# Attention and mixer in one kernel: lead-in reordered, half sums folded in 14 pairs, drains in a row of GpSimd additions

## The chip, the cores and the metric

The kernel runs on one core of a Trainium2 chip. The metric is the device time of one execution in microseconds (us); lower is better. The engines are called as the profile calls them: PE (TensorE), DVE (VectorE), ACT (ScalarE), POOL (GpSimd) and SP (SyncE, which here only issues DMAs).

## The reference

Two blocks follow each other. q, k, v and the centroids are float32.

- Routing attention: 4 batches, 8 heads, 768 tokens, head dimension 64. Each q and each k is assigned to the one of 16 centroids with the greatest cosine; a query sees only the keys of its own cluster.
- An MLP mixer on the heads put side by side (4 x 768 x 512): one product over tokens (768 to 256 and back), then one over channels (512 to 1536 and back), both with a ReLU and a residual.

```python
mask = q_assign[:, :, :, None] == k_assign[:, :, None, :]
scores = np.where(mask, scale * np.matmul(q, k.transpose(0, 1, 3, 2)), -1e9)
attn = softmax(scores)
x = np.matmul(attn, v)                     # (B,H,S,D), then to (B,S,H*D)
h = np.maximum(x.transpose(0, 2, 1) @ w_tok1, 0.0) @ w_tok2
u = x + h.transpose(0, 2, 1)
out = u + np.maximum(u @ w_ch1, 0.0) @ w_ch2
```

`softmax` stands for the reference's exponential of scores less their greatest, divided by its sum. The weights come as 64-bit floats, which the kernel rounds to 32 bits itself.

## The kernel before, in words

**Order of work.** The kernel adds every operation to a `Program` (L77) with the engines that may do it, a cost for each, and the keys it reads and writes. PE's operations stay in the order in which they are added. For the others a planner (L151) goes forward in planned time and gives each engine, out of what is ready, the operation that is due first; `after` is the planned time before which an operation isn't ready. Due times come from PE's own times going back (L138). So the planned times set only the order of each engine's queue; on the chip each queue runs in its order, with semaphores.

**Lead-in.** `begin` (L944) loads the centroids and the q and k of pairs 0 and 1 and two v, makes an identity matrix on POOL, sets constants, and has PE multiply the identity by itself (`keep_busy`, L1024: 11 times here, each two instructions). The centroids are normalised on DVE and ACT (a square root, and behind it an Exp on one column, L984, which makes ACT load its table for Exp), turned by one PE product, and copied to `cbd`; between the turn and the copies stand 5 more dummy products. `turn_qk` (L1029) turns a pair's q and k by 12 PE products with the identity, in three batches of four, each copied from PSUM to SBUF by ACT (L863) or DVE (L865). `route` (L1071) multiplies the turned q and k with the centroids (four products), then DVE transposes (L1088), takes the maximum (L1089), compares, and transposes back (L1093). For pair 0 the result is placed by eight small instructions (L1114, L1118, L1120, L1125) in a mask operand in SBUF; for the others it goes through ACT (L1097, which also adds up the hits) and three DMAs.

**Attention** goes over 16 pairs of heads. `pair` (L1305) does for each: `scores` (L1150), 12 chunks of two products and two mask products in bfloat16, each chunk then taken by ACT's exponential (L1193) out of one of three sets of two PSUM banks; `values` (L1237), six rounds of 16 products; and the softmax's denominators. For these `add_up` (L1201) adds the exponentials of three key blocks to `es[0]` and of the other three to `es[1]`, four DVE additions of 1536 columns. `sums` (L1251) multiplies them by a matrix of ones in the next pair's values, behind the first round: one set of four products for each of `es[0]` and `es[1]`, or one set in all if the two halves were added first. `FOLD` (L52) has a letter for each pair: `-` is two sets, `V` adds the halves on DVE, `T` adds them by a DMA that POOL issues and that adds to its target (no pair has a `T` before). The q and k of pair 3 and later are turned by DMA transposes, not by PE. In pair 0 PE computes three score chunks ahead, then turns pair 1 and routes it, and only then comes to the mask products; pair 2 is turned and routed after the values of pair 0.

Beside attention, DVE rounds the weights piece by piece (`weight_round`, L1336) and forms sums of blocks of them, which go to DRAM. The loads are planned from `START` = 14 us on, `STEP` = 10 us apart.

**Mixer.** Token and channel products are done by a scheme of seven block products instead of eight. The sums of blocks that it needs are formed on DVE and, in the first channel product, on POOL: a long row of additions of 384 columns (`tt`, L881, with `("POOL",)`).

Of the kernel before, what the change touches and what calls it, by code (L numbers as in the profile page):

```python
# [48 lines left out]
SUM_LO, SUM_HI = 1e-15, 1e15  # L49
GRAIN = 32  # L50
CHECK_AT = 532.0
FOLD = "-VVVVVVVVVV-----"  # L52

# [15 lines left out]
SELF = 0.13  # L69
START, STEP = 14, 10  # L70

# [651 lines left out]
def kernel(  # L723
# [43 lines left out]
    def buf(kb, shape, dt=F32):  # L767
        return Buf(arena, int(kb * 256), shape, dt)
# [31 lines left out]
    qkt = [buf(111 + 3 * i, [NQK, P], U16) for i in range(2)]  # L800
    rb = buf(117, [HS], BF16)
    nsq = buf(118, [P])
    mxs = buf(118.5, [32])
# [65 lines left out]
    def halves(dst, src, n, rd, wr, engines=("ACT",), kind="ACT16"):  # L869
# [9 lines left out]
        )  # L879

    def tt(dst, a, b, op, n, rd, wr, engines=("DVE",)):  # L881
        def fn(e):
            (nc.vector if e == "DVE" else nc.gpsimd).tensor_tensor(out=dst, in0=a, in1=b, op=op)  # L883

        return g.add({e: cost(e, n) for e in engines}, fn, rd, wr)

# [57 lines left out]
    def begin():  # L944
# [3 lines left out]
        load_qk(1, 1.0)  # L948
        load_v(0, 12.0)
        load_v(1, 32.0)  # L950
        g.add({"POOL": 1.0}, lambda e: make_identity(nc, ident.ap), [], ident.k())
# [17 lines left out]
        vec(lambda: nc.vector.memset(M0.ap, 0.0), 0.5, [], M0.k())  # L969
        keep_busy(11)  # L970

# [3 lines left out]
        def norm(e):  # L975
# [7 lines left out]

            nc.scalar.activation(out=col(5), in_=lo, func=ACT.Exp, scale=0.0)  # L984
            for it in range(2):
# [13 lines left out]

        g.add({"DVE": 4.0}, norm, cen.k(), sq.k() + nsq.k())  # L1000
        turn(ps[:, 7, 0:P], sq.ap[:, 0:P], sq.k(), bank(7))
        keep_busy(5)
        for i in range(2):
# [24 lines left out]

    def turn_qk(m, banks):  # L1029
        src, T = qks[m % 2], Ts[m % 3]  # L1030
        for n, bk in enumerate(banks):
            for i in range(4):
                a, j = divmod(4 * n + i, NJ)
                a = 1 - a
                turn(
                    ps[:, bk, i * P : (i + 1) * P],
                    src.ap[:, a, j].rearrange("p h d -> p (h d)"),
                    [("qk", m % 2, a, 0), ("qk", m % 2, a, 1)] + src.rows(a, a + 1), bank(bk),
                )

            copy(
                T.ap[:, 4 * n : 4 * n + 4].rearrange("p a t -> p (a t)"), ps[:, bk], 512,
                bank(bk), T.rows(4 * n, 4 * n + 4),
            )
# [26 lines left out]
    def route(m, bk):  # L1071
# [4 lines left out]
        for gr in range(4):  # L1076
# [5 lines left out]
            )  # L1082
        a, e, o = rt[0:3]

        def blocks(t):
# [7 lines left out]
        vec(lambda: nc.vector.transpose(out=o.ap, in_=e.ap), 0.56, e.k(), o.k())  # L1093

        g.add(
            {"ACT": 0.6},
            lambda e: nc.scalar.activation(  # L1097
                out=rb.ap, in_=o.ap, func=ACT.Identity, scale=msc.ap[:, 0:1],
                bias=msc.ap[:, 1:2], accum_out=hits.ap[:, m : m + 1],
            ),  # L1100
            o.k() + msc.k(), rb.k() + [("hits", m)],
        )
# [47 lines left out]
    def scores(m):  # L1150
# [22 lines left out]
        if m == 0:  # L1173
            turn_qk(1, (7, 6, 7))
            load_qkr(3, 26.0)
            route(1, 6)
        for n in range(2 * NJ):
# [4 lines left out]
            for h in range(2):  # L1182
# [5 lines left out]
                    bank(2 * s + h), pos=(64 * h, 0),  # L1188
                )
            ex = st[i]  # L1190
            g.add(
# [113 lines left out]
    def pair(m):  # L1305
# [3 lines left out]
        if m:  # L1309
            next_qk(m)  # L1310
        for i in range(NJ):
            if i == 4 and 1 <= m < NP - 2:
                route(m + 2, 0)
# [11 lines left out]
        if m == 0:  # L1325
            load_v(2)
            turn_qk(2, (1, 2, 3))
            route(2, 0)
            next_qk(m)
# [614 lines left out]


    begin()
    turn_qk(0, (0, 1, 2))
    load_qk(2, 20.0)
    route(0, 3)
# [83 lines left out]
```

## Time and profile before

| | |
|---|---|
| median of 3 runs | 794.08 us (793.72 to 794.26) |
| profiled execution | 794.77 us, span 793.0 us, granted PE clock 0.999 |
| ACT, busy | 461.2 us (58%) |
| weight loads (PEld), busy | 465.4 us (59%) |
| DMA queue of SP | 141.83 MB, 71.4% of 16 engines' span |
| DMA queue of ACT | 0.79 MB |

The span is the time from the first to the last instruction of the profiled execution. A group of the profile names line, engine, operation, what is written and read, the shapes and the count; then come the busy time, the mean duration of one in ns, and the engine's idle time just before the group with what ended it. A row of the chain of waits or of the timeline starts with the start and the length in us. A row of PE's waits gives the time waited in all, how often, and the longest. Almost every buffer is part of one tile, `arena`, in SBUF, and `ps` is PSUM, so groups are told apart by line and shape. Lines such as L844, L883, L863 or L903 are those of helpers (a product, an addition, a copy, a DMA).

### The profile page before, as it was taken

What the parts mean: (1) busy time and instruction counts of PE and PEld (TensorE: products, weight loads), DVE (VectorE), ACT (ScalarE), POOL (GpSimd) and SP (SyncE); (2) the same over time, 40 slices, a digit from 0 to 9 for tenths busy, and PEclk for the clock granted to TensorE, in tenths of its full rate; (3) what the DMA queues carried; (4) which work ended last, traced back from release to release, by engine and by line L of the source; (5) the groups of instructions that cost most, each with busy time, mean ns of one, the idle gap of its engine ahead of it and who ended that gap; (6) DMA issues with size and microseconds to landing.
All of it is one profiled execution on the core that took longest, in us unless ns stands there. A gap on an engine that the chain in (4) does not pass through costs nothing.

```text
span 793.0 us, 15364 instructions
## 1 busy us (share of the span) xinstructions
PE 780.1 (98%) x5983; PEld 465.4 (59%) x5983; DVE 677.5 (85%) x876; ACT 461.2 (58%) x612; POOL 190.2 (24%) x185
## 2 busy tenths in 40 slices
PE   7999999999999999999999999999999999999997
PEld 6666666666666666544555555555555555555554
DVE  6869999999999999999999967899953567799964
ACT  4688898888898875599714367642245204400422
POOL 0000000000000000001264599700186379830000
PEclk9999999999999999999999999999999999999999
DMA  9576769777678953659858999975788844444767
GB/s 214 154 174 164 183 151 232 205 219 203 162 207 183 273 180 113 182 110 224 184 139 246 312 290 258 270 191 123 167 188 179 170 106 102 100 101 106 162 144 178
DMA packets 326576, 143.68 MB, mean 181 GB/s; under 512 B 260192, under 2 KB 322400, under 8 KB 326496
## 3 DMA queue, kind: packets, MB, share of 16 engines
q1 hardware_dynamic: 324128, 141.83, 71.4%
q8 instruction: 49, 0.80, 0.4%
q10 hardware_dynamic: 2368, 0.79, 0.4%
q14 instruction: 31, 0.25, 0.1%
HBM read 91.95 MB, written 28.61 MB: 152 GB/s over the span
## 4 chain that ended last, share of the span: by engine, by line
PE 88%; DVE 5%; ACT 3%; issue 2%; DMA 1%; SPq 0%; POOL 0%; DVEq 0%; POOLq 0%; ACTq 0%
PE ps L844 72%; PE ps L1226 16%; DVE arena L883 4%; ACT arena L873 2%; DMA wd<-arena 1%; ACT arena L1193 1%; DVE arena L865 0%; DVE arena L1360 0%; SPq L903 0%; DVE arena L1363 0%; ACT arena L863 0%; DVE arena L1366 0%; DVE arena L1356 0%; DVE arena L1280 0%; DVE arena L1273 0%
## 5 line engine op out<-in xcount | busy, mean ns | idle before, releaser
L844 PE MATMUL ps<-arena 128*128 128x384 f32 (+5 forms) x2735 | 642.4, 463 | 7.3 <-DVE arena L865 2.7
L844 PEld LDWEIGHTS ps<-arena 128*128 128x128 f32 (+1 forms) x2351 | 342.3, 185 | 252.8 <-issue 59.5
L883 DVE TENSOR_TENSOR arena<-arena 128x1536 f32<-128x1536 f32 (+6 forms) x350 | 370.2, 1079 | 10.5 <-PE ps L1226 2.3
L883 POOL TENSOR_TENSOR arena<-arena 128x384 f32<-128x384 f32 x179 | 189.5, 1094 | 510.8 <-DVE arena L883 379.4
L883 DVE TENSOR_TENSOR arena<-ps,arena 128x384 f32<-128x384 f32 (+3 forms) x227 | 189.6, 845 | 79.4 <-PE ps L844 75.4
L873 ACT COPY arena<-arena 128x768 uint16<-128x768 uint16 x221 | 189.4, 953 | 61.4 <-DMA arena<-arena 31.9
L1193 ACT ACTIVATE arena<-ps 128x768 f32<-128x768 f32 x192 | 150.6, 811 | 31.6 <-PE ps L844 29.9
L1226 PE MATMUL ps<-arena 128*32 128x192 f32 (+1 forms) x3248 | 144.7, 335 | 0.0
L1226 PEld LDWEIGHTS ps<-arena 128*32 128x32 f32 x3248 | 103.8, 110 | 44.0 <-issue 13.9
L863 ACT COPY arena<-ps 128x384 f32<-128x384 f32 (+2 forms) x41 | 29.5, 728 | 120.6 <-PE ps L844 120.4
L890 ACT ACTIVATE arena<-arena 128x1152 f32<-128x1152 f32 (+1 forms) x38 | 39.9, 1075 | 54.9 <-DVE arena L883 54.5
L1888 ACT ACTIVATE arena<-arena 128x768 f32<-128x768 f32 x40 | 38.7, 970 | 32.7 <-DMA arena<-in_moe_w_ch_dram 24.7
L844 PEld LDWEIGHTS <-arena 64*128 64x128 bf16 x384 | 19.3, 94 | 25.0 <-issue 0.6
L1360 DVE SCALAR_TENSOR_TENSOR arena<-arena 128x512 uint32<-128x512 uint32 (+1 forms) x31 | 20.6, 681 | 0.3
L1097 ACT ACTIVATE arena<-arena 128x384 bf16<-128x384 f32 x16 | 11.2, 703 | 16.1 <-issue 16.1
L1366 DVE SCALAR_TENSOR_TENSOR arena<-arena 128x512 f32<-128x512 uint32 (+1 forms) x31 | 20.2, 671 | 0.4
L1356 DVE TENSOR_SCALAR arena<-arena 128x512 uint32<-128x512 uint32 (+1 forms) x31 | 13.2, 435 | 5.8 <-DMA arena<-in_moe_w_tok_dram 5.8
L1273 DVE STREAM_TRANSPOSE arena<-ps 128x768 f32<-128x768 f32 x16 | 15.3, 955 | 0.0
L1363 DVE TENSOR_SCALAR arena<-arena 128x512 uint32<-128x512 uint32 (+1 forms) x31 | 14.4, 483 | 0.3
L865 DVE COPY arena<-ps 128x384 f32<-128x384 f32 (+3 forms) x12 | 8.0, 666 | 4.7 <-PE ps L844 4.6
L1088 DVE STREAM_TRANSPOSE arena<-ps 128x384 f32<-128x384 f32 x16 | 9.2, 575 | 3.1 <-PE ps L844 3.0
L1280 DVE STREAM_TRANSPOSE arena<-ps 128x384 f32<-128x384 f32 x16 | 9.3, 579 | 1.5 <-PE ps L1226 1.2
(58 smaller groups left out, 53.1 us busy)
## 6 DMA issues: line engine op xcount, KB each, us to landing
arena<-wd SPq DMA_DIRECT2D x196, 192.0 KB, 3.0
wd<-arena SPq DMA_DIRECT2D x84, 224.0 KB, 3.2
arena<-in_moe_w_ch_dram SPq DMA_DIRECT2D x96, 128.0 KB, 3.0
arena<-in_moe_w_ch_dram SPq DMA_DIRECT2D x16, 768.0 KB, 6.0
arena<-in_v_dram SPq DMA_DIRECT2D x16, 384.0 KB, 4.7
out_dram<-arena SPq DMA_DIRECT2D x14, 384.0 KB, 3.6
arena<-in_k_dram SPq DMA_DIRECT2D x13, 384.0 KB, 4.0
arena<-in_q_dram SPq DMA_DIRECT2D x13, 384.0 KB, 4.2
```

The costliest lines, as they stand in the source:

```text
L844: nc.tensor.matmul(dst, lhsT=lhsT, rhs=rhs, start=start, stop=stop, tile_position=pos, is_transpose=tr, skip_group_check=True,)
L863: nc.scalar.copy(out=dst, in_=src)
L873: nc.scalar.copy(out=dst, in_=src)
L883: (nc.vector if e == "DVE" else nc.gpsimd).tensor_tensor(out=dst, in0=a, in1=b, op=op)
L890: nc.scalar.activation(out=dst, in_=src, func=ACT.Relu)
L1193: lambda e, ex=ex, s=s, u=u: nc.scalar.activation(out=ex.ap[:, :, u * HS : (u + 1) * HS], in_=ps[:, 2 * s : 2 * s + 2, 0:HS], func=ACT.Exp ...
L1226: nc.tensor.matmul(dst, lhsT=lhsT, rhs=rhs, start=start, stop=stop, tile_position=pos, skip_group_check=True,)
L1273: lambda: nc.vector.transpose(out=x.ap[:, :, cols].rearrange("p j (c d) -> p c j d", d=32), in_=ps[:, 6:8, 0:HS],),
L1360: vec(lambda: nc.vector.scalar_tensor_tensor(out=TT, in0=hi, scalar=0xC0000000, in1=hh, op0=ALU.bitwise_and, op1=ALU.bitwise_or), 0.14 + 0 ...
L1363: vec(lambda: nc.vector.tensor_scalar(out=hh, in0=TT, scalar1=0xFF800000, scalar2=None, op0=ALU.bitwise_and), f, T.k(), h.k())
L1366: vec(lambda: nc.vector.scalar_tensor_tensor(out=ll, in0=lo, scalar=float(2.0**-52), in1=hh.bitcast(F32), op0=ALU.mult, op1=ALU.mult,), 0. ...
L1888: lambda e, i=i, func=func, bias=bias, n=n, hi=hi: nc.scalar.activation(out=hi, in_=hi, func=func, bias=bias, accum_out=wsum.ap[:, i, n : ...
```

## The change

- The lead-in: 12 dummy products instead of 11, and the 5 further ones are gone; the first two batches of pair 0's turns come before the centroid's turn, the third behind it. The Exp that loads the table comes after the copies of these turns. The routing of pair 1 comes behind the third mask product instead of ahead of the first. Pair 0's row of hits has buffers of its own (`o0`, `rb0`) and is planned at 18 us at the earliest. Pair 2 is turned among the values of pair 0, ahead of the fourth round. The loads of pair 2's q and k, of two v, of pair 3's q and k and of the weights are planned earlier.
- `FOLD`: seven pairs (1, 3, ..., 13) have their halves added by DVE and seven (2, 4, ..., 14) by a DMA; pairs 0 and 15 stay as they are.
- POOL: every second addition whose planned end lies between 435 and 475 us is followed by a drain.

```diff
+BUSY, HITS_AT = 12, 18.0
+LULL = (435.0, 475.0)
-FOLD = "-VVVVVVVVVV-----"
+FOLD = "-VTVTVTVTVTVTVT-"
-START, STEP = 14, 10
+START, STEP = 9, 9
...
+    o0, rb0 = buf(194, [HS]), buf(196, [HS], BF16)
...
+    row = 0
     def tt(dst, a, b, op, n, rd, wr, engines=("DVE",)):
         def fn(e):
+            nonlocal row
             (nc.vector if e == "DVE" else nc.gpsimd).tensor_tensor(out=dst, in0=a, in1=b, op=op)
+            if e == "POOL" and LULL[0] <= o.end < LULL[1]:
+                row += 1
+                if row % 2 == 0:
+                    nc.gpsimd.drain()
...
-        load_v(0, 12.0)
-        load_v(1, 32.0)
+        load_v(0, 9.0)
+        load_v(1, 26.0)
...
-        keep_busy(11)
+        keep_busy(BUSY)
...
-            nc.scalar.activation(out=col(5), in_=lo, func=ACT.Exp, scale=0.0)
...
         g.add({"DVE": 4.0}, norm, cen.k(), sq.k() + nsq.k())
+        turn_qk(0, (0, 1, 2), (0, 1))
         turn(ps[:, 7, 0:P], sq.ap[:, 0:P], sq.k(), bank(7))
-        keep_busy(5)
+        turn_qk(0, (0, 1, 2), (2,))
+        g.add(
+            {"ACT": 1.5},
+            lambda e: nc.scalar.activation(out=col(5), in_=col(1), func=ACT.Exp, scale=0.0),
+            nsq.k() + Ts[0].k(), [("table",)],
+        )
...
+        if m == 0:
+            o = o0
...
+        r = rb if m else rb0
         g.add(
-            {"ACT": 0.6},
+            {"ACT": 0.75},
...
-            o.k() + msc.k(), rb.k() + [("hits", m)],
+            o.k() + msc.k(), r.k() + [("hits", m)], after=0.0 if m else HITS_AT,
...
             turn_qk(1, (7, 6, 7))
-            load_qkr(3, 26.0)
-            route(1, 6)
+            load_qkr(3, 18.0)
...
+            if m == 0 and n == ahead - 1:
+                route(1, 6)
...
         for i in range(NJ):
+            if i == 3 and m == 0:
+                turn_qk(2, (1, 2, 3))
...
             load_v(2)
-            turn_qk(2, (1, 2, 3))
             route(2, 0)
...
     begin()
-    turn_qk(0, (0, 1, 2))
-    load_qk(2, 20.0)
+    load_qk(2, 9.0)
     route(0, 3)
```

More of the change, by code (lines that the diff above doesn't have):

```diff
@@ L879, in halves @@
         )
+    row = 0
     def tt(dst, a, b, op, n, rd, wr, engines=("DVE",)):
         def fn(e):
+            nonlocal row
             (nc.vector if e == "DVE" else nc.gpsimd).tensor_tensor(out=dst, in0=a, in1=b, op=op)
-        return g.add({e: cost(e, n) for e in engines}, fn, rd, wr)
+            if e == "POOL" and LULL[0] <= o.end < LULL[1]:
+                row += 1
+                if row % 2 == 0:
+                    nc.gpsimd.drain()
+        o = g.add({e: cost(e, n) for e in engines}, fn, rd, wr)
+        return o
     def relu(dst, src, n, rd, wr, engines=("ACT", "DVE")):
@@ L1027, in keep_busy, with turn_qk @@
             mm(ps[:, 5, 0:P], ident.ap, ident.ap, True, True, 0.22, ident.k(), bank(5))
-    def turn_qk(m, banks):
+    def turn_qk(m, banks, parts=range(3)):
         src, T = qks[m % 2], Ts[m % 3]
-        for n, bk in enumerate(banks):
+        for n in parts:
+            bk = banks[n]
             for i in range(4):
@@ L1093, in route @@
         vec(lambda: nc.vector.transpose(out=o.ap, in_=e.ap), 0.56, e.k(), o.k())
+        r = rb if m else rb0
         g.add(
-            {"ACT": 0.6},
+            {"ACT": 0.75},
             lambda e: nc.scalar.activation(
-                out=rb.ap, in_=o.ap, func=ACT.Identity, scale=msc.ap[:, 0:1],
+                out=r.ap, in_=o.ap, func=ACT.Identity, scale=msc.ap[:, 0:1],
                 bias=msc.ap[:, 1:2], accum_out=hits.ap[:, m : m + 1],
             ),
-            o.k() + msc.k(), rb.k() + [("hits", m)],
+            o.k() + msc.k(), r.k() + [("hits", m)], after=0.0 if m else HITS_AT,
         )
```

## The prediction

> **What bounds the kernel now.** I read the page first, then PE's list of waits, then three stretches, then the chain of waits in the lead-in, and last single rows of the timeline.
>
> ```profile
> span 793.0 us, 15364 instructions
> PE 780.1 (98%) x5983; PEld 465.4 (59%) x5983; DVE 677.5 (85%) x876; ACT 461.2 (58%) x612; POOL 190.2 (24%) x185
> PE 88%; DVE 5%; ACT 3%; issue 2%; DMA 1%; SPq 0%; POOL 0%; DVEq 0%; POOLq 0%; ACTq 0%
> ```
>
> ```profile
> PE ps L844 <- DVE arena L865: 2.7, 3, 0.9
> PE ps L844 <- POOL arena masks.py:199: 1.4, 1, 1.4
> PE ps L844 <- DVE arena L883: 1.2, 3, 0.5
> PE ps L844 <- ACT arena L1193: 0.8, 2, 0.6
> PE ps L844 <- DVE arena L1088: 0.7, 1, 0.7
> ```
>
> ```profile
> 40.00:300.00 260.00, 259.80 (x3727) 161.57 (x3727) 242.69 (x333) 222.64 (x295) 0.00 (x0) 1.00 0.76 196
> 300.00:420.00 120.00, 118.79 (x745) 63.86 (x738) 115.80 (x178) 75.09 (x95) 24.00 (x23) 1.00 0.64 153
> 420.00:785.00 365.00, 365.00 (x1138) 214.78 (x1137) 286.44 (x292) 141.46 (x191) 165.46 (x157) 1.00 0.73 181
> ```
>
> PE is the bound: 780.1 of 793.0 us. The stretches (columns: length, busy PE, weight loads, DVE, ACT, POOL, granted clock, DMA share, GB/s) show where its 13 us of idle time are not: 0.2 us in 40 to 300, 1.2 us in 300 to 420, nothing in 420 to 785. So the idle time lies before 40 us and after 785 us, and the waits say what ended it: copies of turned q and k (L865), exponentials (L1193), the routing transposition (L1088). Two things can shorten this kernel: fewer PE instructions, or a tighter lead-in. DVE is second, with 243 of 260 us in the attention stretch, so work added there can turn into PE waits.
>
> **The change, part by part.**
>
> *Lead-in, first link.* Before, 11 dummy products (two instructions each), the centroid turn, 5 more dummies and the 12 turns of pair 0 make the 45 PE instructions ahead of the first copy. After, it is 12 dummies and 13 turns: 37.
>
> ```profile
> 1.35:7.06 5.71, 5.71 (x26) 5.71 (x27) 1.00 1.05 198
> 7.06:9.36 2.30, 2.29 (x20) 2.05 (x19) 1.00 1.39 221
> 1.92 0.64 SPq L903 DMA_DIRECT2D arena<-in_q_dram  x1
> arena<-in_q_dram SPq DMA_DIRECT2D x5, 192.0 KB, 5.4
> ```
>
> Until 7.06 an instruction takes 5.71/26 = 0.22 us, after it 2.30/20 = 0.115, although the granted clock reads 1.00 in both. If the faster rate comes at the same time, 37 instructions end at 7.06 + 11 x 0.115 = 8.3 instead of 9.36: 1.0 us earlier. The last half of q is issued at 1.92 and lands about 5.4 later, at 7.3; the first turn that reads q is instruction 31, at 7.06 + 5 x 0.115 = 7.6, so the load stays hidden. The centroid turn, its copies and the Exp table load now come beside the turns and stay ahead of their users.
>
> By the Trainium skill's page "TensorE: Matmul & The Clock Gate", Part 1 and Part 4, the array runs at half rate until a window of some 3.4 us was busy, and transposes do not count as busy. The two rates above agree with the first half; by the second, 24 dummy instructions might end before the window does, and the half rate would last. That is the first rival below.
>
> *Lead-in, second link.* From the copy on, the chain of waits and the timeline give the steps.
>
> ```profile
> 9.38 0.70 DVE arena L865
> 10.22 3.70 PE ps L844 x24
> 16.19 1.14 PE ps L844 x10
> 18.22 7.54 PE ps L844 x54
> 25.75 7.94 PE ps L1226 x192
> 33.69 1.47 PE ps L844 x12
> 36.03 0.89 PE ps L844 x8
> 36.94 0.59 DVE arena L1088
> 37.58 7.53 PE ps L844 x53
> ```
>
> ```profile
> 11.13 0.58 DVE L1088 STREAM_TRANSPOSE arena<-ps 128x384 f32<-128x384 f32 x1 [1.06 <-PE ps L844]
> 13.54 0.95 DVE L1120 TENSOR_SCALAR arena<-arena 32x384 bf16<-32x384 f32 x2
> 14.51 0.71 DVE L1125 CAST arena<-arena 32x384 bf16<-32x384 f32 x2
> 33.86 0.98 DVE L1273 STREAM_TRANSPOSE arena<-ps 128x768 f32<-128x768 f32 x1
> 8.87 1.30 SPq L903 DMA_DIRECT2D arena<-in_k_dram  x2
> ```
>
> The first four mask pieces are placed by 14.51 + 0.71 = 15.22, but PE's queue holds the mask products behind the routing of pair 1, which starts at 16.19 and is eight instructions long. After, this routing stands behind the third mask product. With the 1.0 us of the first link the masks are there at 14.2, the first exponential can start near 14.7, the routing goes at 15.0 (once its copy of 0.70 is done) and the fourth score chunk at 15.8 instead of 18.22: 2.4 us earlier. What is late next is that routing itself (0.8 us). The delayed row of hits (0.75 us by the kernel's own cost) falls among ACT's exponentials; PE has two chunks in hand there, so I cost it at nothing, with 0.9 us as its other end.
>
> At the end of pair 0 the 12 turns (1.47 us) move among the values, whose last three rounds take 3 x 7.94/6 = 4.0 us and cover the copies. The wait from 35.16 to 36.03 goes: 0.9 us. Then L1088 stands behind L1273 (0.98 us from the end of the values) rather than behind a routing of 0.89, 0.1 us later. Net 0.8. Lead-in: 2.4 + 0.8 = **3.2 us**, between 0 (if DVE or ACT takes up all of it) and 4.2 (ACT helping to place masks).
>
> The moved loads (pair 2's four transfers, two v loads, two raw loads of pair 3, weight pieces from 9 us every 9 us) go through SP's queue in planned order. It already issues pair 2's k at 8.87, as soon as the turns let go of the buffer, so "9 instead of 20" moves little; an earlier weight piece stands behind that same wait. No PE wait hangs on them: nothing gained, at worst some tenths lost, within the 0.9.
>
> *Half sums.* A pair with added halves needs one set of four products with ones instead of two. Ten pairs have that now, fourteen after. A set is 8 instructions of 384 columns, as much as 16 of the 192 instructions of 192 columns that take 7.94 us: 0.66 us. Four sets: **2.6 us** off PE, which never waits there, so all of it counts as long as the halves are ready.
>
> ```profile
> L883 DVE TENSOR_TENSOR arena<-arena 128x1536 f32<-128x1536 f32 x90 | 156.4, 1747 | 5.4 <-PE ps L1226 2.3 <-ACT arena L1193 0.5 <-PE ps L844 0.2
> 114.95 1.72 DVE L883 TENSOR_TENSOR arena<-arena 128x1536 f32<-128x1536 f32 x1
> 119.50 3.62 DVE L883 TENSOR_TENSOR arena<-arena 128x1536 f32<-128x1536 f32 x2
> 117.92 6.67 DVE L883 TENSOR_TENSOR arena<-arena 128x768 f32<-128x768 f32 x8
> 126.33 0.51 PE L1226 MATMUL ps<-arena 128*32 128x384 f32 x4
> ```
>
> DVE loses the adding of five pairs (2, 4, 6, 8, 10) and gets that of two (11, 13): 3 x 1.75 = 5.2 us less. The seven even pairs get a transfer instead, which no row shows: GpSimd issues it, it adds 768 KB to 768 KB, and PE's product with ones waits for it; behind that product stand the values and scores of the whole next pair. POOL has no work in 40 to 300, so nothing stands behind the issue. On DVE the odd pair's first addition waits for the landing, since the transfer reads its target; DVE starts such additions only after the ones product anyway, so a transfer that is in time for PE is in time for DVE.
>
> ```profile
> arena<-in_moe_w_ch_dram SPq DMA_DIRECT2D x16, 768.0 KB, 6.0
> arena<-in_moe_w_ch_dram SPq DMA_DIRECT2D x96, 128.0 KB, 3.0
> L1363 DVE TENSOR_SCALAR arena<-arena 128x512 uint32<-128x512 uint32 x27 | 13.0, 502 | 0.3
> 449.97 30.16 POOL L883 TENSOR_TENSOR arena<-arena 128x384 f32<-128x384 f32 x31 [2.26 <-DVE arena L883]
> L883 POOL TENSOR_TENSOR arena<-arena 128x384 f32<-128x384 f32 x179 | 189.5, 1094 | 510.8 <-DVE arena L883 379.4
> 493.08 6.86 POOL L883 TENSOR_TENSOR arena<-arena 128x384 f32<-128x384 f32 x7 [0.93 <-PE ps L844]
> ```
>
> The nearest rows: a load of 768 KB lands after 6.0 us, one of 128 KB after 3.0, so a further 768 KB costs 768 x 3.0/640 = 3.6. The transfer takes 6.0 (one pass) to 9.6 us (both operands read); I take 9.6, since two operands are read. The room: in pair 4 the third big addition ends at 116.67 and the ones product starts at 126.33. With the fourth (1.75) right behind the third the room is 7.9 us; where it stands now it ends at 121.3 (first half of the row at 119.50), which leaves 5.0. But the kernel plans the transfer with 9.2 us (2.2 times 768 KB by its own formula, and 5 us), so all four additions get due times some 12 us ahead of the product, and the rows at 117.92 are what they can overtake. I cost the wait at **0**, with the late case as a rival.
>
> By the Trainium skill's "DMA: Bandwidth & Descriptors", "Anatomy of one DMA", a GpSimd transfer takes 2.0 us plus bytes/436e3, an estimate of 3.8 us here (it does not count the second operand); by that none would be late. Against it, "SBUF — State Buffer", "Who interferes with whom", says that GpSimd, which writes the descriptors, is locked out while DVE runs in a 2-port mode. No run here shows it; by it one instruction such as L1363's (0.50 us) is the price, and the sum would stay.
>
> *Drains.* The row at 449.97 is 31 additions in 30.16 us, 0.97 from one to the next, while one lasts 1.09: they overlap by 0.12. About 20 drains fall in its beginning. A drain can cost nothing or as much as a further addition, 0.97; I take the lost overlap, 0.12, since emptying the pipeline is what it does. POOL is then 2.4 us late, of which its own wait for PE at 493.08 takes 0.9. PE has no idle time in 420 to 785, so nothing can be won, and its products never wait for POOL there, so I cost the drains at 0; at 0.97 each POOL would be 19 us late and PE would wait, which I leave to the slow end.
>
> *Sum.* 3.2 + 2.6 = 5.8 us. The profiled execution took 794.77 (span 793.0 and 1.8 around it), which gives 789.0; the median of the three runs, 794.08, gives **788.3**.
>
> **Rivals.** *The half rate lasts.* The 13 turns then cost 0.105 us more each (1.4) and the routing doubles (0.8); 2.2 of the lead-in's 3.2 go: 790.5. For it: fewer dummies. Against it: 37 instructions still run without a break. *The lead-in's gain is given back* by ACT and DVE: only the sums count, 791.5. *Folding does not pay*, because DVE, 97% busy in 300 to 420, becomes the bound in pairs 11 to 14 and the 2.6 us turn into PE waits, so that the change does not do what it says: 790.9. Against it: the 5.2 us that DVE loses earlier. *The transfers land late*, the one that ends on the other side: at PE's ones product, seven times. With 7.9 us of room and 9.6 of transfer each is 1.7 late, 12 in all: 800.2; with 5.0 of room and 6.0 to 9.6 it is 7 to 32 us, 795 to 820. It decides from 5.8/7 = 0.8 us each on. For it: DMA is 76% busy in the stretch. Against it: the due times.
>
> **How the numbers follow.** Forecast 788.3 (its own range 786 to 790): 0.50. Half rate: 0.08. Lead-in given back: 0.12. Folding without pay: 0.09. Late transfers: 0.21, of which 0.05 by so little that the time is within 0.2% (1.6 us, about what can be told from no change). Faster is 0.79, the same 0.05, slower 0.16. The low end, 785.8, is a lead-in of 4.2, 2.6 of sums and the 1.4 us of PE idle in 40 to 420 (8.2 in all); it leaves out some 0.05. The high end, 796.5, takes in all rivals but the later transfers and leaves out some 0.13.
>
> **What would show it.** First link: the turns end near 8.4. Second: the first exponential near 14.7, the second pair's scores near 34.4 instead of 37.58. Sums: 144 instead of 176 instructions of 384 columns on L1226. Transfers: PE's waits list no DMA of the arena, and they land in 10 us or less. Drains: PE without idle time from 415 on. What would make it wrong: a PE wait at the ones products of even pairs, or an instruction rate of 0.22 us past 8 us.

## The result, and the profile after

The changed kernel is slower, where the prediction said faster.

| | before | after |
|---|---|---|
| median, same chip | 794.05 us (793.72 to 794.26, four runs) | 800.9 us (800.29, 800.52, 801.29 and 818.2) |
| ratio | | 1.0084 [1.0064, 1.0104] |
| profiled execution | 794.77 us, span 793.0 | 818.2 us, span 816.3 |

The ratio compares the runs of after without the one of 818.2 us. The profiled execution of after is that one: one of its seven transfers took 20 us, which the other three runs, at 800.3 to 801.3, can't all have had in that length. Read it for kinds of waits; sizes come from the experiments.

The page of after: the totals of the engines, and the shares that the engines have of the chain of waits:

```profile
span 816.3 us, 15320 instructions
PE 785.0 (96%) x5943; PEld 468.2 (57%) x5943; DVE 678.1 (83%) x872; ACT 463.0 (57%) x613; POOL 193.5 (24%) x192
PE 69%; DVE 10%; DMA 7%; ACT 5%; POOL 5%; POOLq 2%; issue 2%; SPq 1%; DVEq 0%; ACTq 0%
```

PE has 40 instructions fewer than before (5943 instead of 5983) and is busy for longer; the chain of waits now runs through DMA and POOL, which had 1% and 0%. The first list shows where PE waits (us in all, times, longest), the second two of the three stretches that the prediction shows of before:

```profile
PE ps L1247 <- DMA arena<-arena: 6.6, 1, 6.6
PE ps L847 <- DVE arena L1107: 6.4, 5, 3.1
PE ps L847 <- issue: 6.2, 1, 6.2
PE ps L847 <- DMA arena<-wdm: 1.8, 1, 1.8
```

```profile
40.00:300.00 260.00, 247.92 (x3598) 155.35 (x3598) 227.11 (x308) 212.41 (x277) 5.31 (x6) 0.98 0.89 204
420.00:785.00 365.00, 358.47 (x1103) 209.44 (x1102) 292.08 (x285) 134.61 (x182) 173.09 (x167) 0.99 0.69 172
```

Two stretches that had next to no idle time have it now: 12 us in 40 to 300 (attention, with the transfers) and 6.5 us in 420 to 785 (the mixer, with the drains). The lead-in did what was forecast; its steps in the timeline and in the chain, and the number of products with ones:

```profile
1.36 7.20 PE L847 MATMUL ps<-arena 128*128 128x128 f32 x37 [1.36 <-POOL arena masks.py:199]
14.83 6.89 ACT L1214 ACTIVATE arena<-ps 128x768 f32<-128x768 f32 x9
34.40 9.96 PE ps L847 x72
L1247 PE MATMUL ps<-arena 128*32 128x384 f32 x144 | 15.3, 507 | 6.6 <-DMA arena<-arena 6.6
```

The 37 instructions end at 8.56 (forecast 8.3), the first exponential starts at 14.83 (14.7), the second pair's scores at 34.40 (34.4; before 37.58), and there are 144 instructions of 384 columns (144). What was lost came later, in two places.

**First place: the transfer that is late for DVE.** DVE's and SP's timelines around the transfer of pair 8, which POOL issues at 188.14:

```profile
191.50 4.24 DVE L889 TENSOR_TENSOR arena<-arena 128x768 f32<-128x768 f32 x7
208.41 4.29 DVE L889 TENSOR_TENSOR arena<-arena 128x1536 f32<-128x1536 f32 x4 [12.67 <-DMA arena<-arena]
```

```profile
188.22 5.17 SPq L919 DMA_TRANSPOSE arena<-arena  x1
193.43 7.13 SPq L914 DMA_DIRECT2D arena<-in_moe_w_ch_dram  x2
200.66 8.86 SPq L919 DMA_TRANSPOSE arena<-arena  x1
```

DVE ends its last work at 195.74 and stands still for 12.67 us: next in its queue is the first addition of pair 9, which writes the buffer that the transfer reads. The transfer lands at 208.3. The transposing DMAs of q and k, issued beside it, hold up SP's queue by 5.2 and 8.9 us at the same time. This one is the extreme case, but all seven transfers have DVE's next pair behind them:

```profile
DVE arena L889 <- DMA arena<-arena: 17.4, 5, 12.7
arena<-arena POOLq DMA_DIRECT2D x7, 768.0 KB, 8.8
```

Five of seven were late for DVE, by 17.4 us in all; the median transfer took 8.8 us. Only one was late for PE (the 6.6 us above). What PE waits for in the other cases is L1107, the routing transposition that stands behind the delayed additions in DVE's queue, or a mask (`wdm`) that comes out of it.

**Second place: the row of additions with the drains.** POOL's, DVE's and PE's timelines and a stretch ahead of the stop's end and one behind it:

```profile
498.47 23.12 POOL L889 TENSOR_TENSOR arena<-arena 128x384 f32<-128x384 f32 x24 [0.16 <-POOL arena L889]
```

```profile
512.70 1.36 DVE L889 TENSOR_TENSOR arena<-ps,arena 128x1152 f32<-128x1152 f32 x1 [0.58 <-PE ps L847]
514.94 7.88 DVE L889 TENSOR_TENSOR arena<-arena 128x1152 f32<-128x1152 f32 x1 [0.88 <-POOL arena L889]
```

```profile
524.65 6.54 PE L847 MATMUL ps<-arena 128*128 128x384 f32 x12 [6.18 <-issue]
```

```profile
515.00:522.00 7.00, 3.47 (x11) 1.71 (x9) 7.00 (x1) 2.15 (x5) 6.60 (x7) 1.00 1.03 243
524.65:529.56 4.91, 4.91 (x8) 2.80 (x9) 3.59 (x5) 3.57 (x7) 0.00 (x0) 0.50 0.46 145
```

One DVE addition of 1152 columns took 7.88 us. It ends 1.2 us behind POOL's row of 24 additions (498.47 + 23.12 = 521.59), which is about the time that the addition takes alone. PE stops for 6.18 us, and in the 4.9 us behind the stop its granted clock is 0.50. PE's wait is put down to "issue", since no single event ended it that the profile shows; it ends 0.1 us after DVE has done the two additions out of PSUM that follow the long one (at 524.55; in e2 below also 0.1 us after them).

### The profile page after: what moved, and what is told of

Same layout as the page of the kernel before. It is cut to its first block, busy times and chain, and to the rows that moved or that the text cites. A ratio compares the mean times of both kernels' runs of the same rounds, so it can differ in the third digit from the quotient of the medians.

```text
span 816.3 us, 15320 instructions
## 1 busy us (share of the span) xinstructions
PE 785.0 (96%) x5943; PEld 468.2 (57%) x5943; DVE 678.1 (83%) x872; ACT 463.0 (57%) x613; POOL 193.5 (24%) x192
## 4 chain that ended last, share of the span: by engine, by line
PE 69%; DVE 10%; DMA 7%; ACT 5%; POOL 5%; POOLq 2%; issue 2%; SPq 1%; DVEq 0%; ACTq 0%
PE ps L847 60%; PE ps L1247 9%; DVE arena L889 7%; POOL arena L889 5%; DMA arena<-arena 4%; ACT arena L1214 3%; POOLq L893 2%; ACT arena L876 1%; DMA arena<-wdm 1%; SPq L914 1%; DMA arena<-in_v_dram 1%; DVE arena L1382 1%; DMA arena<-in_q_dram 1%; DVE arena L1388 1%; ACT arena L866 0%
## 5 line engine op out<-in xcount | busy, mean ns | idle before, releaser
L847 PEld LDWEIGHTS ps<-arena 128*128 128x128 f32 (+2 forms) x2343 | 344.4, 186 | 264.7 <-issue 67.9
L889 DVE TENSOR_TENSOR arena<-arena 128x1536 f32<-128x1536 f32 (+6 forms) x347 | 371.7, 1091 | 33.2 <-DMA arena<-arena 17.4
L889 POOL TENSOR_TENSOR arena<-arena 128x384 f32<-128x384 f32 x179 | 186.6, 1069 | 215.9 <-DMA arena<-wd 72.6
L866 ACT COPY arena<-ps 128x512 f32<-128x512 f32 (+2 forms) x43 | 30.6, 724 | 119.7 <-PE ps L847 119.6
L1236 POOL DMA_DIRECT2D arena<-arena x7 | 6.2, 881 | 314.5 <-DVE arena L1301 314.5
L1117 ACT ACTIVATE arena<-arena 128x384 bf16<-128x384 f32 x16 | 11.2, 703 | 11.6 <-issue 11.6
L1107 DVE STREAM_TRANSPOSE arena<-ps 128x384 f32<-128x384 f32 x16 | 9.1, 571 | 2.9 <-PE ps L847 2.6
L868 DVE COPY arena<-ps 128x384 f32<-128x384 f32 (+2 forms) x10 | 6.5, 647 | 5.5 <-PE ps L847 5.5
```

The lines of the kernel that those rows point to most:

```text
L847: nc.tensor.matmul(dst, lhsT=lhsT, rhs=rhs, start=start, stop=stop, tile_position=pos, is_transpose=tr, skip_group_check=True,)
L866: nc.scalar.copy(out=dst, in_=src)
```

## The experiments

My theory after this reading was: (A) the drains make POOL late, so that its row loses the gaps in which DVE's additions got in, and PE stops; (B) a transfer is late for DVE's next pair, not for PE. Rivals: the drains only show up a lateness that comes from the transfers; the transfers cost by their traffic, whoever waits; DVE is the bound.

### The drains

`e2_drains_alone`: the kernel before with the drains.

```diff
+LULL = (435.0, 475.0)
 ...
+            if e == "POOL" and LULL[0] <= o.end < LULL[1]:
+                row += 1
+                if row % 2 == 0:
+                    nc.gpsimd.drain()
```

> The kernel before with only the drains added; the order of every queue stays that of before. Theory A: POOL's row ends some 3 us later, DVE is held out near 500 us, PE waits several us there and its clock falls: 799 to 804 us. Theory B: the drains cost PE nothing: 794 us.

Measured: 802.44 us (802.12 to 803.35), ratio 1.0108 [1.0089, 1.0127]. The timelines of POOL (two of the drained pairs, then the rest of the row), DVE and PE, and the stretch behind the stop:

```profile
469.92 1.96 POOL L887 TENSOR_TENSOR arena<-arena 128x384 f32<-128x384 f32 x2 [0.16 <-issue]
472.05 1.97 POOL L887 TENSOR_TENSOR arena<-arena 128x384 f32<-128x384 f32 x2 [0.16 <-issue]
...
478.44 27.94 POOL L887 TENSOR_TENSOR arena<-arena 128x384 f32<-128x384 f32 x29 [0.16 <-issue]
```

```profile
499.71 7.88 DVE L887 TENSOR_TENSOR arena<-arena 128x1152 f32<-128x1152 f32 x1 [0.19 <-POOL arena L887]
```

```profile
509.43 7.05 PE L845 MATMUL ps<-arena 128*128 128x384 f32 x14 [5.49 <-issue]
```

```profile
509.43:514.07 4.64, 4.64 (x8) 2.52 (x9) 3.32 (x4) 4.58 (x9) 0.00 (x0) 0.50 0.03 6
```

The drains alone make the whole stop, without transfers or a new lead-in. A drained pair comes every 472.05 - 469.92 = 2.13 us; two additions of the row before take 2 x 0.97, so a drain costs 0.2 us. Before, the row had breaks from 480 us on (0.40, 0.93 and 0.95 us, where POOL waited for ACT and PE; the prediction quotes the middle one). With POOL some 3 us late nothing is left to wait for: 29 additions follow without a break until 506.38, and DVE's addition from 499.71 ends at 507.59. The price is 5.49 us of stop and 4.64 us at a clock of 0.50 (2.3 us): 7.8, beside 8.6 by the ratio.

`e10_drains_all_along`: the same, with every second addition of the whole row drained.

```diff
-LULL = (435.0, 475.0)
+LULL = (435.0, 600.0)
```

> The kernel before with the drains of the change, but on after 475 us of planned time to 600, so that POOL's row has a gap of 0.2 us at every second addition to its end. Theory A (DVE is held out only while POOL's additions follow each other without a gap): DVE's addition near 500 us takes 1.4 to 3.5 us instead of 7.9, and the PE wait of 5.5 us falls under 2: 794 to 797 us. Rival: it is POOL's lateness itself on which PE waits, which is greater here: 803 us or more.

Measured: 795.22 us (794.82 to 796.36), ratio 1.0017 [1.0008, 1.0026].

```profile
502.30 1.36 DVE L887 TENSOR_TENSOR arena<-arena 128x1152 f32<-128x1152 f32 x1 [2.27 <-POOL arena L887]
505.50 10.68 PE L845 MATMUL ps<-arena 128*128 128x384 f32 x32 [1.05 <-POOL arena L887]
```

More drains, POOL later still, and the stop shrinks from 5.49 to 1.05 us: the 0.16 us break behind each drained pair lets DVE's addition in, and it takes 1.36 us again. So it isn't POOL's lateness as such that costs 8.6 us, but that it leaves a row without a break where DVE's addition comes.

A row without a break is not enough, though. In e14 (below), which has no drains, DVE's addition comes to such a row too, and gets in after one of POOL's additions:

```profile
491.92 19.12 POOL L889 TENSOR_TENSOR arena<-arena 128x384 f32<-128x384 f32 x14 [1.15 <-ACT arena L901]
498.74 2.15 DVE L889 TENSOR_TENSOR arena<-arena 128x1152 f32<-128x1152 f32 x1
```

The same holds in e4, e5, e8 and e12 (1.82 to 2.09 us). The long hold stands in four profiles, those of the kernels whose drains stop at 475 us (after, e0, e2, e3: 7.87 or 7.88 us each). In these four DVE had been idle for 0.19 to 0.91 us, waiting for a result of POOL's row; in the other five its own previous instruction ran until then. Whether that is the condition was not tested. (In e10 DVE stood idle too, and the break let it in.) In all four DVE came when seven additions of the row were left, so "until the row ends" and "for seven additions" can't be told apart.

`e3_old_fold` (the changed kernel with drains and lead-in, `FOLD` of before) and `e6_lead_in_alone` (the same without the drains):

```diff
-FOLD = "-VTVTVTVTVTVTVT-"
+FOLD = "-VVVVVVVVVV-----"
-LULL = (435.0, 475.0)
+LULL = (0.0, 0.0)          (e6 alone)
```

> The changed kernel with the letters of before (ten pairs folded by DVE, no transfers), drains and lead-in as changed. Theory C: planning the four big additions early enough for a transfer pushes the routing on DVE back, and PE waits for it (1.3, 0.4, 0.7 us) and for a mask transfer (1.8 us, and 1.7 us of lower clock): with the old letters these waits go and the four sets of sums (2.6 us) come back, 800.9 + 2.6 - 5 = 798 to 799 us. Rival: the transfers cost nothing by themselves, and the old letters only bring the sums back: 803 us.

> The changed kernel without drains and with the letters of before: the lead-in and the earlier weight loads alone. The prediction's first term: 794.2 - 3.2 = 791.0 us, pair 1's scores near 34 us. Rival: the lead-in's gain is given back later by DVE or the loads: 793 to 794.5 us.

Measured: e3 799.34 us (798.91 to 799.67), ratio 1.0064 [1.0046, 1.0083]; e6 791.73 us (791.38 to 792.13), ratio 0.9973 [0.9964, 0.9983]. With the drains it is 7.6 us more (e3 above e6; 7.2 by the ratios, as the two ran on different chips). The lead-in is worth 2.4 us by e6 and 3.1 by e3 beside e2.

### The transfers

`e1_no_drains`: the changed kernel without the drains.

```diff
-LULL = (435.0, 475.0)
+LULL = (0.0, 0.0)
```

> The changed kernel without its drains. Theory A: the drains make POOL's row of additions late (0.2 us each, 17 of them, from the profile of the changed kernel), so that the row is still running without a gap when DVE comes to its next addition of two SBUF operands; DVE then gets no turn until the row ends, and PE waits 6.2 us and runs at the lower clock for 6.8 us after it. Without the drains that goes: 800.9 - 6.2 - 2.4 = 792 us, and PE has no idle time between 440 and 780 us. Theory B: the meeting of the row and DVE's addition comes from the moved plan and not from the drains: 800 to 801 us, with the same PE wait.

Measured: 796.09, 800.32, 806.57 and 820.71 us, ratio 1.0117 [1.0065, 1.0168]. The stop near 500 is gone, as theory A has it, but not the time, which I had expected at 792: it is no faster than with the drains. So the transfers alone are enough to undo the change, and the times scatter. The profile is of the fastest run; what the slower ones lost beyond it is not on record. PE's waits, DVE's waits, and DVE around the transfer issued at 187.50:

```profile
PE ps L847 <- DVE arena L1107: 5.4, 4, 1.9
PE ps L847 <- DMA arena<-wdm: 2.1, 1, 2.1
```

```profile
DVE arena L889 <- DMA arena<-arena: 6.2, 4, 2.4
```

```profile
190.87 4.23 DVE L889 TENSOR_TENSOR arena<-arena 128x768 f32<-128x768 f32 x7
197.25 4.29 DVE L889 TENSOR_TENSOR arena<-arena 128x1536 f32<-128x1536 f32 x4 [2.15 <-DMA arena<-arena]
...
204.38 5.30 DVE L889 TENSOR_TENSOR arena<-arena 128x1536 f32<-128x1536 f32 x3
209.59 0.57 DVE L1107 STREAM_TRANSPOSE arena<-ps 128x384 f32<-128x384 f32 x1
```

This is the usual case. PE never waits for a transfer. DVE does, 2.15 us, with nothing else left that it may do; then it works without a break to 209.59, where the routing is late, and PE waits 1.21 us for it.

`e4_new_fold_alone`: the kernel before with the new `FOLD` alone.

> The kernel before with only the new letters. Theory C: the sums save 2.6 us, waits for the routing and the mask transfers take 3 to 6 us: 794 to 798 us, with PE waits for L1088 between 100 and 310 us. Rival (the prediction's own sum): 794.05 - 2.6 = 791.5 us and no PE waits there.

Measured: 804.36, 804.53, 816.9, 822.01 and 825.92 us, ratio 1.0129 [1.0105, 1.0153]. The fold alone costs 10 us or more, where I had expected 4 at most. In its profile (of the run of 816.9) one transfer took 18.5 us, and weights come late besides (2.9 us of PE at `arena<-wd`); this kernel loads them later than the changed one does, but whether that is why was not tested.

`e5_all_by_dve`: no drains, and DVE adds the halves of all 14 pairs.

```diff
-FOLD = "-VTVTVTVTVTVTVT-"
+FOLD = "-VVVVVVVVVVVVVV-"
```

> The changed kernel without drains and with all fourteen pairs added by DVE (no transfers). If drains and transfers hold the whole loss, both gains of the prediction stand here: 794.2 - 3.1 - 2.6 = 788.5 us, and no PE wait for the routing or a mask transfer between 100 and 310 us. Rival: DVE, 97% busy from 300 us on, becomes the bound with four more additions (7 us): 790 to 793 us, with PE waits for DVE between 250 and 450 us.

Measured: 801.17 us (800.32 to 802.07), ratio 1.0093 [1.0078, 1.0109]. PE's waits:

```profile
PE ps L847 <- DVE arena L889: 4.5, 5, 1.9
PE ps L847 <- DMA arena<-wd: 4.0, 1, 4.0
```

That is above both ranges. PE has no wait between 100 and 310 us, but DVE, with four additions more than in e6, gets its weight work done late, and the sums of weight blocks reach PE late. So DVE can't take over what the transfers do.

`e7_small_transfers` and `e8_traffic_no_wait` tell DVE's wait from the traffic. In e7 a transfer moves 16 columns instead of 1536, with the plan unchanged; most of the half sum of the even pairs is left out. e8 is e7 with a transfer of full size behind each, on a buffer (`idle`, set to zero at 40 us of planned time) that nobody uses.

```diff
-                a.ap.rearrange("p h t -> p (h t)"), b.ap.rearrange("p h t -> p (h t)"),
+                a.ap.rearrange("p h t -> p (h t)")[:, 0:16], b.ap.rearrange("p h t -> p (h t)")[:, 0:16],
 ...                                                  (from here on e8 alone)
+        flat = idle.ap.rearrange("p h t -> p (h t)")
+        g.add(
+            {"POOL": 1.0},
+            lambda e: nc.gpsimd.dma_start(flat, flat, accum_op=ALU.add),
+            [("half", m, 0), ("half", m, 1)], idle.k(), (16, 6144),
+        )
```

> The changed kernel without drains; each of the seven transfers adds 16 columns instead of 1536 (so most of the half is left out of the sums), with every queue's order and all planned times as they are. Theory C1: the PE waits for the routing (1.4, 1.2, 1.9 us) come from DVE's order, in which the four big additions stand ahead of the routing: they stay, and only the mask transfer's wait (2.1 us) and the scatter between runs go: 792 to 794 us, runs within 1 us. Theory C2: the waits come from the transfers' load on the DMA engines: all go, 788 to 789 us.

> The kernel of e7 (no drains, transfers of 16 columns, so most of the half sum is left out in the even pairs), and behind each small transfer GpSimd issues one of the full size, 768 KB added to 768 KB, on a buffer that no other instruction reads or writes. So the traffic is that of e1 and no instruction waits for it. If what costs is that VectorE's next additions stand at the head of its queue and wait for the landing, the loss doesn't come back: 788 to 790 us and no PE wait of over 0.5 us between 100 and 310 us. If what costs is the traffic itself (the transposing DMAs beside it get slower and q, k or masks come late), the loss comes back without the wait: 796 us or more and PE waits for L1107 or for the mask's transfer, as in e1. Between the two, the part that comes back is the traffic's part.

Measured: e7 788.48 us (788.3 to 788.98), ratio 0.9935 [0.992, 0.995]; e8 790.33 us (789.89 to 791.05), ratio 0.9956 [0.9941, 0.9971]. The stretch from 40 to 330 us in e1, e7 and e8:

```profile
40.00:330.00 290.00, 283.38 (x4167) 178.73 (x4166) 265.61 (x359) 233.98 (x307) 6.18 (x7) 1.00 0.82 203
```

```profile
40.00:330.00 290.00, 290.00 (x4184) 181.01 (x4181) 272.96 (x371) 238.41 (x312) 6.17 (x7) 1.00 0.71 186
```

```profile
40.00:330.00 290.00, 288.61 (x4183) 180.64 (x4180) 271.32 (x365) 236.95 (x311) 12.36 (x14) 1.00 0.84 205
```

PE idles 6.6 us in e1, not at all in e7 and 1.4 us in e8, whose DMA share is the highest of the three (0.84). e7 takes away wait and traffic together; its time is the one that theory C2 gave, but e8 shows that the load of the DMA engines is not the main reason. The traffic costs some 2 us (e8 above e7). The rest of e1's loss goes with the wait.

`e9_planned_longer` tells the planner of a transfer of twice the size, so that it puts the waiting additions later in DVE's queue.

```diff
-        g.add({"POOL": 1.0}, fn, a.k() + b.k(), a.k(), (2.2 * 768 * 1024, 6144))
+        g.add({"POOL": 1.0}, fn, a.k() + b.k(), a.k(), (4.4 * 768 * 1024, 6144))
```

> The changed kernel without drains, with full transfers, whose planned size goes from 2.2 to 4.4 times 768 KB: the planned landing comes 7 us later (14 instead of 7 us after the issue), so the planner puts other work ahead of the additions that wait for the landing. If VectorE's waits at the head of its queue are the cause, they go and the time comes down from e1's 796 to 803 us to 789 to 791. If the traffic is the cause, the time stays at 796 us or more. If the room was the cause all along (a ones product that comes too early), the longer plan changes nothing at PE and the time also stays.

Measured: 813.51 us (810.31 to 820.97), ratio 1.0237 [1.0203, 1.027]: this is slower than e1, for which none of the three theories has a reason. PE's largest wait and SP's queue around 125 us:

```profile
PE ps L847 <- DMA arena<-wdm: 9.3, 5, 3.2
```

```profile
127.65 3.42 SPq L914 DMA_DIRECT2D arena<-in_moe_w_ch_dram  x4
131.12 0.93 SPq L914 DMA_DIRECT2D arena<-wdm  x2
```

The planner takes the DMA engines for occupied while a transfer lasts, and moves SP's queue as well: four weight loads now stand ahead of the mask's transfers, and PE waits for masks. The edit changed two things, so it says nothing on the theories. `e14_planned_later` moves the planned landing alone (7.0 to 11.2 us behind the issue):

```diff
-        g.add({"POOL": 1.0}, fn, a.k() + b.k(), a.k(), (2.2 * 768 * 1024, 6144))
+        g.add({"POOL": 1.0}, fn, a.k() + b.k(), a.k(), (2.2 * 768 * 1024, 6144), more=4.2)
```

> As e9 (the planner is told a later landing of the transfers, 11.2 instead of 7.0 us behind the issue), but without telling it that the DMA engines are taken for longer, which in e9 moved weight loads in SyncE's queue ahead of the masks' transfers and the transposes. If e9's loss came from that order: 789 to 793 us here, with VectorE's waits for a DMA of the arena under 2 us in all. If a later place of the additions itself makes VectorE late for the routing: 796 us or more, with PE waits for L1107 or for the mask's transfer.

Measured: 793.14 us (790.38 to 796.91), ratio 0.9989 [0.9975, 1.0003]. DVE's waits for transfers are gone, and with them all of PE's waits in attention but one, 2.7 us for a mask at 288 us. The transfers themselves are as long as in most profiles (8.2 to 10.0 us, pair 14's apart). By the ratios (1.0117 and 0.9989) some 10 us of e1's loss come back by the planned landing alone; the intervals allow 5 to 15. The median lies 0.1 us above the range that I gave, with one mask late; two of the ten runs, at 790.4, come close to e8.

`e12_third_buffer` takes the wait away with the transfers complete: it has a third buffer of 6 KB (per partition), in rotation for pairs 1 to 11. `e13_third_fewer` also leaves pairs 12 and 13 at two sets of products, so that no transfer is left that DVE waits for.

```diff
-    es = [buf(84 + 6 * i, [2, S]) for i in range(2)]
+    es3 = [buf(at, [2, S]) for at in (84, 90, 200)]
+    es_of = [(0, 1)] + [((0, 1), (2, 0), (1, 2))[(m - 1) % 3] for m in range(1, 12)] + [(1, 0)] * 4
 ...
+        es = [es3[i] for i in es_of[m]]          (in add_up and in sums)
 ...
-FOLD = "-VTVTVTVTVTVTVT-"
+FOLD = "-VTVTVTVTVTV--T-"          (e13 alone)
```

> The changed kernel without drains, complete, with a third buffer of 6 KB that pairs 1 to 11 use in rotation with the two of before: the halves of a pair are then added up in a buffer that the transfer of the pair before neither reads nor writes, for the first half of them, and in the buffer that it read for the second half, some 7 us later. So full transfers and their traffic stay and the wait at the head of VectorE's queue goes (it stays in pair 13, behind pair 12's transfer). If that wait is the cause: 789 to 791 us, PE waits of over 0.5 us at most near 300 us, and no run over 795. If the transfers cost by their traffic or by being stuck, whoever waits: 796 us or more, with waits between 130 and 290 us as in e1.

> The kernel of e12 without the added halves of pairs 12 and 13 (two sets of products more, 1.3 us), so that no transfer is left that VectorE waits for. If pair 13's wait (1 to 2 us, and what follows from it) is all that is left in e12: the same time within 1 us, 789 to 791 us. If e12 is far above 791 for another reason, this one is above it by 1.3 us.

Measured: e12 796.22 us (794.68 to 812.25), ratio 1.0051 [1.0022, 1.008]; e13 789.0 us (788.91 to 789.3), ratio 0.994 [0.9927, 0.9953]. The stretch from 40 to 330 us of e13, and PE's waits for weights in e12:

```profile
40.00:330.00 290.00, 290.00 (x4202) 181.71 (x4199) 274.46 (x375) 240.99 (x313) 5.32 (x6) 1.00 0.82 206
```

```profile
PE ps L848 <- DMA arena<-wd: 6.2, 2, 5.4
```

e13 has six full transfers and e1's DMA share of 0.82, and PE doesn't idle for a moment in attention: with a buffer that lets DVE go on, a transfer of 6.1 to 8.5 us costs nothing. The third buffer also moves the transfers: they now leave 2.1 to 2.6 us ahead of the transposing DMAs, not with them, and are shorter than e1's 8.3 to 10.4 us. So the wait alone is told from the rest by e8 and e14, not by this pair. Of e12 my expectation was wrong (796 instead of 789 to 791, and three of twelve runs over 805). In 40 to 330 us it is nearly as good as e13 (PE busy 289.6 of 290; DVE waits 1.2 us for one transfer), but PE stops for 5.4 us, until 508.84, for sums of weight blocks that come back from DRAM late, as in e5. e12 differs from e13 by the half sums of pairs 12 and 13 alone, so those set off the stop; but e1 has them too and has no such stop, so how they do it stays open. e13 comes out where I had put it only for an e12 as fast.

`e13` beats the kernel before by 0.6%, and of the complete kernels it is the fastest. Beside e6 it has two sets of products fewer (1.3 us) and gains 2.7 us; where the rest comes from stays open.

`e11_last_pair_only`: e6 and one transfer, in pair 14.

```diff
-LULL = (435.0, 475.0)
+LULL = (0.0, 0.0)
-FOLD = "-VTVTVTVTVTVTVT-"
+FOLD = "-VVVVVVVVVV---T-"
```

> The changed kernel without drains, with the old folding of pairs 1 to 10 by VectorE and one transfer alone, in pair 14, beside which no transposing DMA runs (this pair's transfer took 6.0 us in every profile so far). By the theory that late landings are the price, this one costs nothing and saves one set of products with ones, 0.66 us: 791.1 us against 791.7 of e6. By the rival that a transfer costs more than a set wherever it stands: 792 us or more.

Measured: 792.3 us (791.66 to 792.81), ratio 0.9981 [0.9972, 0.999]. The transfer took 5.9 us and nobody waited for it, but the 0.66 us don't show. The median lies where the rival has it (792 or more); since the interval overlaps e6's, 0.9973 [0.9964, 0.9983], the two are not told apart.

`e0_after_again`: the changed kernel as it is, for a second profile.

> The changed kernel as it is, for a profile of one of its usual executions near 800.5 us: the profile shown first has a transfer that took 20 us. By the theory: a stop of PE of 5 to 6 us and a half clock behind it between 500 and 530 us (8 us, from the drains), and stops of 1 to 3 us between 130 and 310 us (4 to 6 us together, from transfers that land after VectorE's next addition is due), with no transfer over 11 us.

Measured: 812.39 and 802.75 us, ratio 1.0175 [1.0119, 1.0232]. The profile is of the first; PE's and DVE's waits:

```profile
PE ps L847 <- DVE arena L1107: 7.5, 5, 4.7
PE ps L847 <- issue: 6.2, 1, 6.2
```

```profile
DVE arena L889 <- DMA arena<-arena: 12.9, 6, 7.0
```

The stop of 6.2 us and the waits for L1107 are there again, these longer than I had expected (4.7 us the longest). My limit of 11 us for a transfer did not hold: pair 8's took 14.5.

## Why the prediction was wrong

- **Lead-in, 3.2 us: right.** Each step came within 0.3 us of its forecast (rows above), and alone it is worth 2.4 to 3.1 us of the whole. In e6 0.9 us is given back at 390 to 412 us, where PE waits 1.4 us for DVE and waited 0.5 before. The first rival, that the half rate lasts, did not come true: the 37 instructions end at 8.56.
- **Half sums, 2.6 us: right in kind and size.** With the landing out of the way, e7 is 3.2 us below e6, and at 788.48 where the sum of the prediction stands (788.3). e7 leaves out most of the adding, so this is the size of the term, not a kernel to use; and the single set of e11 did not show.
- **Transfers, costed at 0: wrong.** The step that failed is "so a transfer that is in time for PE is in time for DVE". The duration was well taken (8.8 us median, 9.6 forecast) and the room for PE's product was there (13.4 to 14.0 us from issue to product). But the reason given, "DVE starts such additions only after the ones product anyway", does not hold, and the trace of before shows it. There, the ones product of pair 5 ends when the denominators' transposition (L1280) gets it:

```profile
138.69 3.61 DVE L883 TENSOR_TENSOR arena<-arena 128x1536 f32<-128x1536 f32 x2
...
146.61 0.58 DVE L1280 STREAM_TRANSPOSE arena<-ps 128x384 f32<-128x384 f32 x1 [0.24 <-PE ps L1226]
147.12 5.30 DVE L883 TENSOR_TENSOR arena<-arena 128x1536 f32<-128x1536 f32 x3
```

Three of pair 6's five additions follow the product, but the first two, into `es[0]`, stand 8 us ahead of it: nothing reads `es[0]` any more. A transfer does read it, until it lands. The planner puts those two behind the planned landing, 7 us after the issue (in e7, where they need not wait, DVE comes to them 7.5 to 8.0 us after it), and DVE's queue runs in order. What the transfer takes longer (0.8 to 2.4 us in e1, more if it is held up) stops DVE, which has little slack (272.96 of 290 us busy in e7), and, through the routing, PE.
- **Drains, costed at 0: wrong twice.** One costs 0.2 us, not 0.12. More to the point, "its products never wait for POOL there" looked only at what PE waits for. POOL and DVE disturb each other. The Trainium skill's page "SBUF — State Buffer", section "Who interferes with whom", says that a DVE instruction with two inputs in SBUF contends with a GpSimd instruction that reads SBUF, and that the ports that they share are an exclusive lock. The runs agree on the pair: in after, the addition with an operand in PSUM took 1.36 us beside the row, the one with both in SBUF 7.88. On the length they split: in e4, e5, e8, e12 and e14 DVE was held for less than one addition of POOL, in after, e0, e2 and e3 for seven.
- **The rivals.** "The transfers land late", 0.21, had the sign, and its 800.2 us lies close to the 800.9. But its place was PE's ones product, which was late once in seven in the profile of after; the closeness is luck, since in the same profile the drains' stop and the half clock behind it take 8.6 us (6.18 and half of 4.91), for which no rival stood. "Folding does not pay" (DVE becomes the bound) is what e5 shows if DVE takes all 14 pairs.
- **The two losses don't add up.** The drains alone cost 8.6 us, the transfers alone 8 to 18 (the three shorter runs of e1 above e7), and both together 12 above e7. How the two share what is lost was not separated.

Open: why a transfer and the transposing DMAs beside it sometimes take 14 to 20 us (pair 8 in both profiles of after, pair 6 in e4). In these three cases POOL issued the transfer 0.1 to 0.2 us ahead of the first transposing DMA, in most of the others with the old buffers 0.2 to 0.7 us behind it; but in e9 a transfer of 15.5 us was issued behind it, so the order is not shown to be the cause.

## What to carry to other kernels

When work moves from an engine to a DMA, look for the next instruction that writes one of its buffers, not only for the one that reads its result: in a queue that runs in order it holds up all behind it. A further buffer (e13) or a later place in the queue (e14) takes that wait away without a faster transfer. An engine for which no product waits can still set the time by holding up another: before delaying a row of GpSimd additions, see which VectorE additions with both operands in SBUF come in its breaks, and whether VectorE would then stand waiting for the row.

## What was not expected of the hardware

- A row of GpSimd additions without a break can hold a VectorE addition of two SBUF operands until the row ends, seven additions long: 7.87 or 7.88 us instead of 1.36, in four profiles (after, e0, e2, e3). In five others (e4, e5, e8, e12, e14) the addition got in after at most one of GpSimd's (1.82 to 2.15 us); what decides is not shown. A break of 0.16 us was enough to let it in (e10). Additions with one operand in PSUM were not held (1.36 us).
- A drain behind every second GpSimd addition cost 0.2 us (e2).
- A stop of 5.5 us cost PE as much as 7.8: the granted clock was 0.50 in the 4.6 us behind it (e2).
- A DMA that adds 768 KB to 768 KB in SBUF took 5.7 to 6.4 us with no transposing DMA beside it (pair 14, all profiles), 6.3 to 10.4 with one or two, and 13 to 20 in five cases.
